# Gated spectral mix: t transform in four 32-row tiles, inverse d transform in two 64-row tiles, no regroupings, Mish table first, a new order

## The chip, the cores and the metric

The kernel runs on one core of a Trainium2 chip. The metric is the time of one execution in microseconds (us), the median of the runs; the profile is of one execution, and its times are told from the start of its span. TensorE (PE) multiplies, VectorE (DVE), ScalarE (ACT) and GpSimd (POOL) do the rest, and transfers (DMA) are issued from the queue of SyncE (SP) or of ACT. TensorE writes to PSUM, eight banks of 128 x 512 float32, and one of the other engines has to evict a bank before it can be written anew.

## What is computed

With S = 2048, D = 512, F = 1792 and one batch, all inputs in bfloat16:

```python
x = A_x
g = sigmoid((x * gate_w).sum(-1, keepdims=True))
X = rfft2(x.astype(float32), axes=(-2, -1)) * (A_w_r + 1j * A_w_i)     # 2048 x 257 filter weights
a = irfft2(X, s=(S, D), axes=(-2, -1)).astype(bfloat16)
h = einsum("bsd,df->bsf", x, B_w1) + B_b1
act = h * tanh(softplus(h))                                            # Mish
b = einsum("bsf,fd->bsd", act, B_w2)
return g * a + (1 - g) * b
```

(B_x is not used: the second branch takes x as well.)

## The kernel before

**Two branches, one written order.** Every step is a task with a name, made with `G.add` or `dma`; `ORDER` (L325) lists all tasks by name in one order, with the engine and the PSUM bank or scratch slot of those that have a choice (`t4_0::4` begins at bank 4, `sw4_0:dve:0` runs on DVE in slot 0). `place` (L219) deals them out to five queues in this order, and `emit` gives each task a wait for what it reads, and for what the last user of its bank or slot did. So each engine works off its queue strictly in the order of the text. The estimated durations in the code play no part in the program. A task of POOL also waits for the last DVE task marked `lock` that stands ahead of it in the order.

**Dense branch.** `m{c}_{ft}` (L853): for each of four chunks c of 512 rows and each of 14 feature tiles ft, four matmuls with 512 columns fill a bank, and ACT evicts it with Mish (`h{c}_{ft}`, L858). `n{t}` (L871): for each of 16 row tiles, 14 matmuls with 512 columns; `o{t}` (L885, L888) evicts them with the factor 1 - g. The transposed x that the m tasks read comes for tiles 0 to 7 from TensorE (`tr{t}`, `evx{t}`) and for 8 to 15 from transposing transfers (`xt{t}`).

**Spectral branch.** Rows are split as s = 16 p + t, and the 2-D transform is made in three products and back in three:

- butterflies of the two halves of d: `bf{a}_{uv}` (L574), on DVE or POOL;
- `p{t}` (L587): the transform over p, four 128-column matmuls for each t, evicted by `ep{t}` into `zu` (rC);
- `d{t}` (L598): the transform over d, likewise, evicted by `ed{t}` into rD;
- first regrouping: `s1w{g}` writes rD to a scratch in memory (four transfers of 512 KB), `s1r{g}` reads it back into `In` (rE), regrouped so that the 128 partitions hold (t, e, real or imaginary, c);
- `t{q}_{i}` (L705): the transform over t: for each of 64 slots f one matmul, 128 rows, with a matrix `Mm[:, f, :]` of its own (rF, loaded by `ldM{g}`); evicted by `et{q}` into `Y` (rC);
- the filter, for each group q of 8 slots: `sw{q}_{j}` copies Y with its partition halves swapped (L715, L716), `p1`, `p2`, `ad` (L723, L726, L729) multiply with `Wr` (rW) and `Wi` (rA) and add;
- the column k = 0 and the Nyquist column share one place; the products `e1` (L745, L746) and `e2` (L765, L767) and the small tasks es0, es1, xp1, xp2, ead, e3 filter them apart. `e1` reads all filtered groups of Y;
- `it{q}_{i}` (L783): the inverse over t, with `Gm` (rB, `ldG{g}`), evicted by `eit{q}` into `H` (rF);
- second regrouping: the twelve copies `hx` from `Hv` (rF) to `Dv` (rC), so that the 128 partitions hold both real and imaginary parts;
- `id{t}` (L827): the inverse over d, four matmuls with 128 rows for each t, evicted by `ec` (L834, L835) and two sums `ey` (L838) into `yb`;
- `ip{t}`: the inverse over p; for tiles 8 to 15 it is added in the bank of `n{t}` (L879, with g and 1/(1 - g) folded into its matrix, `rfs`), for 0 to 7 it has a bank of its own (L897) and `fin{t}` (L901) adds it.

**Filter weights.** `wr0s1`, `wi1s0` and the like load pieces of the 2048 x 257 weights from SP's queue to rS; eight moves for each of Wr and Wi (`wrm000` and so on, L638 on ACT, L640 and L641 on DVE or POOL), each of 32 partitions and 16 slots, put them in their layout, contiguous over k; `wrn0`, `wrn1` copy rW to its other half by a transfer, `win0`, `win1` (L651) do the same for Wi on DVE with a change of sign; `wrc`, `wrz`, `wic`, `wiz` set the shared column.

**The gate.** `gate0` and `gate8` (L676): 32 matmuls of one column each; `zcl`, `ez` (POOL), `ezb`, `ez1`, `omg`, `gc` make g and 1 - g. `zt` (L804) transposes a small piece of it, `zte` evicts that, and `zw`, `zr` spread it through memory.

Of the kernel before, what the change touches and what calls it, by code (L numbers as in the profile page):

```python
# [8 lines left out]
BF = mybir.dt.bfloat16  # L9
# [9 lines left out]
WP = 130  # L19
# [111 lines left out]
def _build_consts():  # L131
    R, FDm = _const_p(), _const_d()
    M, G = _const_t()
    front = np.concatenate([R[:, None, :], FDm], axis=1)
    inv = np.zeros((128, 5, 128))
    inv[:, 0] = R.T * (2.0 / (S * D))
    for uv in range(2):
        for e in range(2):
            for kri in range(2):
                inv[kri::2, 1 + 2 * uv + e] = FDm[:, 2 * uv + e, 64 * kri:64 * kri + 64].T  # L140
# [4 lines left out]
    return dict(front=front, inv=inv, edge=np.concatenate(edge, axis=1),  # L145
                M=M.transpose(1, 0, 2), G=G.transpose(1, 0, 2))
# [179 lines left out]
warm::0 wrp1 graw wrp0 x0 ones ident braw x2 ebase cRF w1_0 tr0::0 bf0_0:dve bf0_1:dve tr_b::1 tr1::2 evx0:act xt8 ev_b tr3::3 bf2_0:dve cFD bf2_1:dve  # L326
tr2::0 evx3:dve evx1:act p0::4 x4 evx2:dve p1 p2::6 ep0:act p3 m0_0::0 ep2:dve xt11 m0_2::1 h0_0 m0_1::6 w1_8 h0_2 bf4_1:dve tr7::7 h0_1 tr4::1 tr6::0
evx7:dve tr5::4 bf4_0:pool evx6:act d2::2 evx4:dve d3 evx5:dve wr1s1 m0_3::7 ed2:dve m1_1::6 h0_3 p4::2 w1_4 h1_1 p6::4 m0_13::7 m1_13::6 h0_13 wr0s2
p7 wr1s0 h1_13 m1_11::7 ep6:dve wr0s0 m0_11::6 h1_11 m1_6::4 h0_11 xt13 m0_7::5 wrm100:act wrm101:dve x8 m0_8::6 wrm111:dve wrm110:dve m0_5::7 xt9 h0_8
p5 h0_7 d6::0 ep4:dve d7 wi1s1 h0_5 m1_9::6 ed6:act bf8_1:pool m1_12::7 xt14 h1_9 d0::0 m0_4::5 h1_12 h1_6 ldM2 m0_10::7 bf8_0:dve h0_4 p8::2 x12 h0_10  # L330
p9 m1_8::5 ep8:dve d1 h1_8 m0_12::7 wi1s0 ed0:act d8::4 d9 p10::2 wr0s1 h0_12 p11 d4::0 m1_10::6 ep10:act bf12_1:dve gate0::7 ed8:act bf12_0:pool s1w0
d10::2 h1_10 zcl0 d11 m1_3::4 ed10:dve d5 h1_3 m0_6::6 ez0 ed4:dve wi0s1 wrm010:act wim111:pool p14::4 p15 m1_0::7 ez10 ep14:dve s1w1 p12::0 h1_0 p13
m0_9::2 ezb0 ep12:dve wip1 h0_6 wrm000:pool d14::4 wim100:act d15 m1_4::3 omg0 ed14:dve xt10 d12::0 d13 wip0 m1_7::6 h1_4 wrm011:dve s1w2 h0_9 m1_2::7
wrm001:dve h1_7 gc0 wim110:dve m1_5::2 ed12:act wim101:pool m2_0::6 xt12 h1_2 h1_5 m2_8::0 s1w3 m2_11::7 win1 m2_13::1 wic1:pool m2_7::2 s1r2 wiz1:dve
m2_2::3 wi0s0 m2_10::4 h2_11 m2_3::5 wi0s2 h2_13 s1r0 h2_2 m2_12::7 h2_7 m2_5::1 xt15 h2_12 wim010:dve h2_0 m2_6::2 wim011:dve h2_3 s1r3 m2_4::3 h2_6
wim001:dve s1r1 h2_5 m2_9::5 wim000:pool h2_4 gate8::1 h2_9 wrn0 h2_10 m3_13::3 zcl8 h2_8 win0 m3_2::2 h3_13 ldM0 m3_5::0 h3_2 wic0:pool wiz0:dve ez8
t4_0::4 ldG1 h3_5 t4_1 m3_3::2 ezb8 ez18 wrc0:pool et4:act omg8 wrz0:pool m3_11::3 w2_2 h3_3 sw4_0:dve:0 t1_0::4 sw4_1:dve h3_11 t1_1 m3_9::2 p2_4:dve
et1:act zt::3 t5_0::0 ldM1 zte m3_12::6 h3_9 sw1_1:act:1 t0_0::2 t0_1 zw m3_8::7 et0:dve h3_12 ldG2 sw1_0:act m3_6::4 sw0_1:dve:2 ldM3 h3_8 m3_10::5
p1_1:dve sw0_0:act p2_1:dve t2_0::6 t2_1 w2_0 m3_4::2 h3_6 ad_1:dve w2_8 h3_10 p1_0:dve m3_0::3 h3_4 p2_0:dve t3_0::4 h3_0 t3_1 et2:dve m3_7::2 ldG3
m2_1::3 et3:dve ad_0:pool h3_7 t6_0::6 h2_1 t6_1 wrn1 t5_1 sw2_0:dve:1 t7_0::4 sw3_1:act:2 sw2_1:dve t7_1 n3_0::3 et6:dve p1_2:pool et7:act zr rft  # L340
sw3_0:act inv et5:act p2_2:dve ldG0 n0_0::2 wrc1:dve o3_0:dve wrz1:pool edge rfs p1_4:dve ad_2:dve ad_4:dve sw7_1:act:1 n1_0::3 p1_3:dve sw5_0:act:0
sw7_0:dve p2_3:dve sw5_1:act p2_7:dve ad_3:dve o0_0:act n7_0::0 p2_5:dve sw6_1:act:2 p1_5:dve sw6_0:dve ad_5:dve p2_6:dve p1_6:dve n4_0::2 o7_0:act
p1_7:dve ad_6:dve ad_7:dve o1_0:dve e1::0 n2_0::3 o4_0:act xp1::1 es0::2 es1 xp2 ead::0 e2::2 m3_1::0 o2_0:act e3 it1_0::2 h3_1 it1_1 it0_0::4 eit1:dve
it0_1 it7_0::6 eit0:act it7_1 it3_0::0 it3_1 eit7:dve it5_0::2 eit3:act it5_1 it2_0::4 it2_1 eit5:act eit2:dve it4_0::6 it4_1 it6_0::0 it6_1 n5_0::2
eit6:act eit4:dve hx8_00 hx8_10 hx8_01 n6_0::3 o5_0:act hx8_11 hx0_01 hx4_11 hx4_10 hx0_00 id14::6 o6_0:dve id15 hx0_11 id12::0 ec14:act:0 id13 id10::4
# [8 lines left out]
def _build(nc, A_x, A_w_r, A_w_i, B_x, B_w1, B_b1, B_w2, gate_w, out, merge=8, xtp=8, NWARM=13):  # L354
# [6 lines left out]
    scr = nc.dram_tensor("scr", (NT, 4, 128, 128), BF)  # L361
# [4 lines left out]
    with es:  # L366
# [17 lines left out]
        wsr = sb("wsr", [128, 2, NF], BF)  # L384
        wsi = sb("wsi", [128, 2, NF], BF)
# [61 lines left out]
        scr_w = scr.rearrange("t r m k -> m (t r) k")  # L447
        scr_r = scr.rearrange("t r (c f) k -> (t r c) (f k)", c=2)
# [8 lines left out]
        def dma(name, dst, src, us, cls="dma", queue="sp", is_out=False, transpose=False, **kw):  # L457
# [7 lines left out]
            issue = 1.31 if transpose else dict(sp=0.6, act=0.4, pool=1.1)[queue]  # L465
            t = G.add(name, [(queue, issue, fn)], cls, **kw)
# [45 lines left out]
        G.add("warm", [("pe", NWARM * 0.213, f_warm)], "warm", writes=[wb])  # L512
        G.add("ones", [("pool", 0.2, lambda e: e.memset(identt[:, :], 1.0))], "small", writes=["ident"])
# [14 lines left out]
        for ri, (src, nm) in enumerate(((A_w_r, "wr"), (A_w_i, "wi"))):  # L528
            wv = src.rearrange("(q m) k -> q m k", m=128)
            for fh in range(2):  # L530
# [6 lines left out]
                for j, (pm, fs, ms, us) in enumerate(parts):  # L537
                    dma(f"{nm}{fh}s{j}", sg[pm:32:2, fs, :], wv[:, ms, :], us, writes=[(nm, fh, "s", j)])
# [40 lines left out]
        for t in range(0, NT, 2):  # L579
            b, b2 = _Buf("b2"), _Buf("b2")  # L580
            for i in range(2):
                def f_p(e, t=t + i, i=i, b=b):
# [8 lines left out]
            evac(f"ep{t}", lambda t=t: zu[:, :, t:t + 2, :], lambda b=b: pair(b).rearrange("p (t c f) -> p c t f", t=2, c=4), 1024,  # L591
                 [b], [("zu", t), ("zu", t + 1)], "p")
            for i in range(2):
                def f_d(e, t=t + i, i=i, b=b2):
                    ins = None
                    for c in range(4):
                        o = 256 * i + 128 * (c % 2)
                        ins = e.matmul(bank(b, c // 2)[:, o:o + 128], zu[:, c, t, :], FD[:, c, :], start=True, stop=True)  # L598
# [13 lines left out]
        dma("edge", rD[:, 7168:8192], d_edge[:].rearrange("p c m -> p (c m)"), 0.7, writes=["edge"], deps=t_s1w)  # L612
        for g in range(4):
            dma(f"ldM{g}", Mm[:, 16 * g:16 * g + 16, :], d_M[:, 16 * g:16 * g + 16, :], 1.4, writes=[("M", g)])
# [344 lines left out]
```

## Time and profile before

| | |
|---|---|
| median of 3 runs (lowest to highest) | 142.3 us (142.06 to 142.41) |
| span of the profiled execution, first to last instruction | 139.5 us |
| the time that lies around the span, from these two | 2.8 us |
| granted TensorE clock, mean | 1.000 |
| busy: PE, DVE, ACT, POOL | 128.4, 80.2, 79.6, 25.3 us |
| L853 (m), 224 matmuls of 512 columns | 52.1 us |
| L871 (n), 210 matmuls of 512 columns and 28 of 256: the groups that read hs, rD, rS | 24.9, 12.7, 12.9 us |
| L587, L598, L705, L783, L827, 64 matmuls of 128 columns each | 4.9, 5.2, 4.7, 4.1, 4.6 us |
| transfers | 23.57 MB in 23,870 packets |

Busy time of PE is the time in which at least one matmul is under way by the profile; single matmuls overlap (379 ns is the mean of one with 512 columns, and 216 ns the distance between the starts of two). The profiled execution has no time of its own beside its span; the median stands 2.8 us above it.

### The profile page before, as it was taken

What the parts mean: (1) busy time and instruction counts of PE and PEld (TensorE: products, weight loads), DVE (VectorE), ACT (ScalarE), POOL (GpSimd) and SP (SyncE); (2) the same over time, 40 slices, a digit from 0 to 9 for tenths busy, and PEclk for the clock granted to TensorE, in tenths of its full rate; (3) what the DMA queues carried; (4) which work ended last, traced back from release to release, by engine and by line L of the source; (5) the groups of instructions that cost most, each with busy time, mean ns of one, the idle gap of its engine ahead of it and who ended that gap; (6) DMA issues with size and microseconds to landing.
All of it is one profiled execution on the core that took longest, in us unless ns stands there. A gap on an engine that the chain in (4) does not pass through costs nothing.

```text
span 139.5 us, 2328 instructions
## 1 busy us (share of the span) xinstructions
PE 128.4 (92%) x918; PEld 70.0 (50%) x918; DVE 80.2 (58%) x121; ACT 79.6 (57%) x107; POOL 25.3 (18%) x27
## 2 busy tenths in 40 slices
PE   7989999999699996989959999499999999999992
PEld 5646445676344434454434444147648565444451
DVE  0665359529973034347993498945905669972220
ACT  3496699889980696989895069117714144000111
POOL 3023006089515005710361000000000000000000
DMA  4999999995959999999999500000075310050142
GB/s 106 300 309 227 252 214 171 350 192 130 212 114 249 237 162 335 303 370 280 310 305 215 194 5 0 0 5 0 0 297 192 136 37 1 5 207 18 75 153 94
DMA packets 23870, 23.57 MB, mean 169 GB/s; under 512 B 13940, under 2 KB 19956, under 8 KB 23540
## 3 DMA queue, kind: packets, MB, share of 16 engines
q1 hardware_dynamic: 23392, 23.20, 63.0%
q10 hardware_dynamic: 468, 0.23, 0.8%
q8 instruction: 7, 0.11, 0.3%
q14 instruction: 3, 0.02, 0.1%
HBM read 15.02 MB, written 4.20 MB: 138 GB/s over the span
## 4 chain that ended last, share of the span: by engine, by line
PE 52%; DMA 19%; DVE 12%; ACT 7%; SPq 6%; issue 2%; ACTq 0%
PE ps L871 24%; PE ps L853 14%; DMA rW<-rW 9%; DMA rF<-c_m 8%; SPq L463 5%; ACT tmp L716 3%; PE ps L827 3%; DMA w_sb<-in_B_b_dram 2%; PE ps L598 2%; DVE rC L729 2%; DVE rF L493 2%; DVE rD L493 2%; DVE rC L493 2%; PE ps L587 2%; ACT hs L858 1%
## 5 line engine op out<-in xcount | busy, mean ns | idle before, releaser
L853 PE MATMUL ps<-rX,w_sb 128*128 128x512 bf16 x224 | 52.1, 379 | 0.0
L853 PEld LDWEIGHTS ps<-rX,w_sb 128*128 128x128 bf16 x224 | 20.8, 98 | 21.2 <-ACT hs L858 0.4
L871 PE MATMUL ps<-w_sb,hs 128*128 128x512 bf16 x112 | 24.9, 379 | 2.0 <-ACT rC L496 1.8
L885 ACT ACTIVATE rX<-ps,omg 128x512 bf16<-128x512 f32 (+1 forms) x11 | 7.1, 648 | 26.2 <-PE ps L879 19.9
L858 ACT ACTIVATE hs<-ps,b1f 128x512 bf16<-128x512 f32 x28 | 18.2, 692 | 4.4 <-PE ps L853 4.3
L871 PEld LDWEIGHTS ps<-w_sb,hs 128*128 128x128 bf16 x112 | 10.7, 98 | 15.2 <-ACT rC L496 2.0
L493 DVE CAST rC<-ps 128x1024 bf16<-128x1024 f32 x10 | 12.1, 1221 | 7.6 <-PE ps L587 6.1
L716 ACT ACTIVATE tmp<-rC 64x1024 bf16<-64x1024 bf16 x9 | 9.5, 1055 | 6.4 <-DVE rC L729 6.2
L871 PE MATMUL ps<-w_sb,rS 128*128 128x512 bf16 (+1 forms) x70 | 12.9, 336 | 0.0
L871 PE MATMUL ps<-w_sb,rD 128*128 128x512 bf16 x56 | 12.7, 379 | 0.0
L858 ACT ACTIVATE rD<-ps,b1f 128x512 bf16<-128x512 f32 x14 | 8.4, 689 | 4.5 <-DMA scr<-rD 3.2
L858 ACT ACTIVATE rS<-ps,b1f 128x512 bf16<-128x512 f32 x14 | 9.3, 687 | 2.5 <-PE ps L853 2.3
L574 POOL TENSOR_TENSOR rB<-rA 128x1024 bf16<-128x1024 bf16 x3 | 6.4, 2120 | 21.8 <-DVE rB L574 11.7
L838 DVE TENSOR_TENSOR rA<-tmp,ps 128x512 bf16<-128x512 f32 x16 | 9.9, 682 | 0.4 <-PE ps L827 0.4
L888 DVE TENSOR_SCALAR rX<-ps,omg 128x512 bf16<-128x512 f32 x6 | 4.5, 748 | 8.6 <-PE ps L871 4.9
L871 PEld LDWEIGHTS ps<-w_sb,rS 128*128 128x128 bf16 x70 | 6.7, 98 | 4.8
L871 PEld LDWEIGHTS ps<-w_sb,rD 128*128 128x128 bf16 x56 | 5.5, 98 | 6.6 <-DVE rX L901 0.2
L574 DVE TENSOR_TENSOR rB<-rA 128x512 bf16<-128x512 bf16 (+1 forms) x7 | 5.0, 740 | 4.9 <-DMA rA<-in_A_x_dram 4.9
L834 ACT ACTIVATE tmp<-ps 128x512 f32<-128x512 f32 x7 | 4.0, 598 | 6.7 <-PE ps L827 6.6
L901 DVE SCALAR_TENSOR_TENSOR rX<-ps,gcol,rX 128x512 bf16<-128x512 f32 x8 | 5.6, 745 | 2.5 <-PE ps L897 2.5
L496 ACT ACTIVATE rC<-ps 128x1024 bf16<-128x1024 f32 x6 | 6.1, 1020 | 0.8 <-PE ps L705 0.4
L726 DVE TENSOR_TENSOR tmp<-tmp,rA 128x1024 bf16<-128x1024 bf16 x8 | 6.2, 787 | 0.1
(86 smaller groups left out, 144.3 us busy)
## 6 DMA issues: line engine op xcount, KB each, us to landing
w_sb<-in_B_w_dram SPq DMA_DIRECT2D x3, 768.0 KB, 8.1
rF<-c_m SPq DMA_DIRECT2D x4, 512.0 KB, 9.3
scr<-rD SPq DMA_DIRECT2D x4, 512.0 KB, 4.2
rE<-scr SPq DMA_DIRECT2D x4, 512.0 KB, 8.1
rB<-c_g SPq DMA_DIRECT2D x4, 512.0 KB, 9.4
out_dram<-rX SPq DMA_DIRECT2D x7, 256.0 KB, 2.0
rA<-in_A_x_dram SPq DMA_DIRECT2D x3, 512.0 KB, 8.5
rW<-rW SPq DMA_DIRECT2D x2, 520.0 KB, 11.4
```

The costliest lines, as they stand in the source:

```text
L463: return e.dma_start(a, b)
L493: return e.tensor_copy(out=o(), in_=i())
L496: return e.activation(o(), i(), AF.Copy)
L574: return e.tensor_tensor(out=xu[:, a:b_, uv, :], in0=x_sb[:, a:b_, 0:256], in1=x_sb[:, a:b_, 256:512], op=ALU.add if uv == 0 else ALU.subt ...
L716: ("act", act(1024), lambda e, z=z, lo=lo, i_=i_: e.activation(tb(z)[lo:lo + 64], i_, AF.Copy))],
L726: return e.tensor_tensor(out=zv(z), in0=zv(z), in1=Wi[:, fa:fb, 0:128], op=ALU.mult)
L838: return e.tensor_tensor(out=yb[:, t:t + 2, 256 * h:256 * h + 256].rearrange("p t (i e) -> p t i e", e=2), in0=t4(z), in1=o4(bank(b, 1)), ...
L853: ins = e.matmul(bank(b), w1_sb[:, dt_, 128 * ft:128 * (ft + 1)], xT[:, c, dt_, :, :], start=(dt_ == 0), stop=(dt_ == 3))
L858: G.add(f"h{c}_{ft}", [("act", act(512, 1), lambda e, c=c, ft=ft, b=b: e.activation(hs[c][:, ft, :], bank(b), AF.Mish, bias=b1f[:, ft:ft + ...
L871: ins = e.matmul(bank(b)[:, 0:hi - lo], hs[c][:, ft, 128 * tl:128 * (tl + 1)], w2_sb[:, ft, lo:hi], start=(ft == 0), stop=(ft == NFT - 1 a ...
L885: return e.activation(bs[:, t, lo:hi], bank(b)[:, 0:hi - lo], AF.Copy, scale=omg[:, t:t + 1])
L901: return e.scalar_tensor_tensor(out=bs[:, t, :], in0=bank(b), scalar=gcol[:, t:t + 1], in1=bs[:, t, :], op0=ALU.mult, op1=ALU.add)
```

## The change

- The rows of `In` are now (j, c, t) with j = f mod 4: each of the four 32-row tiles of the array takes one slot f, and what was one matmul of 128 rows for a slot is four of 32 rows, added up in the bank over a = (e, real or imaginary). A task `t{q}` has 64 matmuls for 16 slots and four banks, in the order g, a, j, so that neighbours go to different tiles and banks: 256 in all for 64 before. In this layout the transform over d can write it directly: `p` is evicted into `zu` with t innermost (`ep`), `d{g}` takes 128 columns of (8 slots of f, 16 t) and is evicted by `ed{g}` into `In`. `s1w`, `s1r` and the scratch are gone. A `d` task now reads what all `ep` tasks wrote.
- `id{t}` reads `Hv` where `it` left it: eight matmuls of 64 rows in two row tiles, for four of 128 rows. The `hx` copies are gone.
- A one-element Mish (`tab`) is the first task of ACT, and every Mish eviction depends on it.
- The moves of the filter weights write their columns regrouped (k u to u k, 132 columns a slot in place of 130), and read every second element for that. Four POOL memsets (`wrp`, `wip`) and the copies to `wsr`, `wsi` are gone; the shared column sits in column 65.
- `c0{q}`, four small DVE copies, keep the unfiltered shared column, and `e1` reads them; `e3` is written in four parts.
- Seven of the ten filter loads are issued from ACT's queue, the other three from SP's.
- `ORDER` is new: x0, x2, x4, x8 are loaded ahead of w1, the m tasks of all chunks lie around and behind the t tasks (23 of them between `t3` and `e1`), and n, id and ip follow.

The core of the diff (the two orders are cut down to their beginnings and the stretch around the t tasks, and the constants, which only follow the layout, are left out):

```diff
-WP = 130
+WP = 132
...
-warm::0 wrp1 graw wrp0 x0 ones ident braw x2 ebase cRF w1_0 tr0::0 bf0_0:dve bf0_1:dve tr_b::1 tr1::2 evx0:act xt8 ev_b tr3::3 bf2_0:dve cFD bf2_1:dve
...
-m2_1::3 et3:dve ad_0:pool h3_7 t6_0::6 h2_1 t6_1 wrn1 t5_1 sw2_0:dve:1 t7_0::4 sw3_1:act:2 sw2_1:dve t7_1 n3_0::3 et6:dve p1_2:pool et7:act zr rft
...
+x0 tab warm::0 ones ident x2 x4 bf0_1:dve tr0::1 bf2_0:pool tr2::2 evx2:dve cRF x8 graw tr3::3 braw w1_0 evx0:act bf4_0:pool evx3:act bf2_1:dve tr1::4
...
+m0_7::6 p5 ep4:act gate0::7 m0_6::3 m1_7::1 wr0s0:sp h0_7 bf12_1:dve h1_7 ebase zcl0 ez0 p8::4 m0_1::2 h0_1 wr0s1:act wr1s0:act wrm001:pool p9 p12::6
+p13 ep8:dve p14::0 wr1s1:act ldM0 p15 ep14:dve m1_6::2 m1_2::4 m0_9::5 ezb0 wrm101:pool ep12:act d2::0 d3 ed2:dve d4::6 h0_6 h1_6 h1_2 xt14 d12::2 d5
...
+wrm000:dve m1_13::5 m1_12::0 h1_12 m2_13::3 h2_13 et01:dve c00 m2_8::4 gate8::1 wim010:dve zcl8 ez8 h1_13 wim001:dve ldM2 win0 wrn0 sw01_1:dve:0
+wrc0:pool ldM3 t1::62 et11:act et10:act m1_1::0 h1_1 h2_8 m2_11::5 sw00_1:dve:1 h2_11 m3_1::1 m3_2::2 wrm100:dve t2::63 et21:act c01 m3_5::0 m1_8::5
+m2_1::3 wim110:dve wic0:pool wrn1 wim101:dve h3_2 ezb8 zt::4 win1 et20:act zte h1_8 sw00_0:dve ez18 sw01_0:dve h3_1 wrz0:dve m0_11::2 h0_11 t3::64
...
+        t_tab = G.add("tab", [("act", 1.4, lambda e: e.activation(junk[:, :], one[:, 0:1], AF.Mish))], "small", writes=["junk"])
...
-                    dma(f"{nm}{fh}s{j}", sg[pm:32:2, fs, :], wv[:, ms, :], us, writes=[(nm, fh, "s", j)])
+                    dma(f"{nm}{fh}s{j}", sg[pm:32:2, fs, :], wv[:, ms, :], us, queue="sp act", writes=[(nm, fh, "s", j)])
...
-            evac(f"ep{t}", lambda t=t: zu[:, :, t:t + 2, :], lambda b=b: pair(b).rearrange("p (t c f) -> p c t f", t=2, c=4), 1024,
+            evac(f"ep{t}", lambda t=t: zu.rearrange("p u f t -> p (u f) t")[:, :, t:t + 2], lambda b=b: pair(b).rearrange("p (t x) -> p x t", t=2), 1024,
...
-                    for c in range(4):
-                        o = 256 * i + 128 * (c % 2)
-                        ins = e.matmul(bank(b, c // 2)[:, o:o + 128], zu[:, c, t, :], FD[:, c, :], start=True, stop=True)
+                    o = bank(b, i).rearrange("p (e r u k) -> p u e r k", e=2, r=2, u=2)
+                    for uv in range(2):
+                        for e_ in range(2):
+                            c = 2 * uv + e_
+                            ins = e.matmul(o[:, uv, e_], rC[:, 2048 * c + 128 * g:2048 * c + 128 * (g + 1)], FD[:, c, :].rearrange("p (r k) -> p r k", r=2), start=True, stop=True)
...
-            t_s1w.append(dma(f"s1w{g}", scr_w[:, 16 * g:16 * g + 16, :], rD[:, 2048 * g:2048 * (g + 1)].rearrange("p (r k) -> p r k", k=128),
-                             2.4, "s1", reads=[("y1", 4 * g + i) for i in range(4)], writes=[("scr", g)]))
-        for g in range(4):
-            t_s1r.append(dma(f"s1r{g}", rE[g:128:4, :], scr_r[32 * g:32 * g + 32, :], 1.4, "s1", reads=[("scr", g)], writes=[("In", g)]))
...
-                            i_ = sg[:, 16 * h:16 * h + 16, 0:129] if pt == 0 else sg[:, 16 * h:16 * h + 16, 256:127:-1]
-                            o_ = dstv[base + 32 * pt:base + 32 * pt + 32, f0 + 16 * h:f0 + 16 * h + 16, 0:129]
+                            i_ = sg[:, 16 * h:16 * h + 16, 0:WP] if pt == 0 else sg[:, 16 * h:16 * h + 16, 256:256 - WP:-1]
+                            i_ = i_.rearrange("p f (k u) -> p f u k", u=2)
+                            o_ = dstv[base + 32 * pt:base + 32 * pt + 32, f0 + 16 * h:f0 + 16 * h + 16, :].rearrange("p f (u k) -> p f u k", u=2)
...
-                    for k in range(4):
-                        f = f0 + 4 * i + k
-                        ins = e.matmul(bank(b, i)[:, 128 * k:128 * (k + 1)], Mm[:, f, :], In[:, f, :], start=True, stop=True)
+                for g in range(4):
+                    for a in range(4):
+                        for j in range(4):
+                            r = slice(32 * j, 32 * j + 32)
+                            ins = e.matmul(bank(bp[j // 2], j % 2)[:, 128 * g:128 * g + 128], Mm[r, 4 * q + g, a, :], In[r, 4 * q + g, a, :],
+                                           start=(a == 0), stop=(a == 3))
...
-        G.add("e1", [("pe", 0.2, f_e1)], "edge", reads=yall + ["edge"], writes=[eb])
+        G.add("e1", [("pe", 0.2, f_e1)], "edge", reads=[("c0s", q) for q in range(4)] + ["edge"], writes=[eb])
...
-                    dma(f"hx{a}_{uv}{kri}", Dv[kri:128:2, uv, a:b_], Hv[uv:128:2, kri, a:b_], 0.3 * (b_ - a) / 4 + 0.1, "hx",
...
-                    for uv in range(2):
-                        for e_ in range(2):
-                            o = 256 * i + 128 * e_
-                            ins = e.matmul(bank(b, uv)[:, o:o + 128], Dv[:, uv, t, e_, :], cinv[:, 2 * uv + e_, :], start=True, stop=True)
+                    for e_ in range(2):
+                        o = 256 * i + 128 * e_
+                        for kri in range(2):
+                            for uv in range(2):
+                                r = slice(64 * uv, 64 * uv + 64)
+                                ins = e.matmul(bank(b, uv)[:, o:o + 128], Hv[r, kri, t, e_, :], cinv[r, 2 * kri + e_, :], start=(kri == 0), stop=(kri == 1))
...
-            dph = {0: [], 1: [], 2: t_s1w, 3: t_mv}[c]
+            dph = [t_tab] + (t_mv if c == 3 else [])
```

More of the change, by code (lines that the diff above doesn't have):

```diff
@@ L330 @@
[L330 to L337, printed above, removed]
@@ L342 @@
[L342 to L345, printed above, removed]
@@ L383, in _build @@
         tmp = sb("tmp", [128, 3, 1024], BF)
[L384 to L385 removed]
+        c0s = sb("c0s", [128, NF], BF)
         b1f = sb("b1f", [128, NFT], F32)
@@ L610, in _build @@
[L610 to L614 removed]
+            dma(f"ldM{g}", Mm[:, 4 * g:4 * g + 4, :, :], d_M[:, 4 * g:4 * g + 4, :, :], 1.4, writes=[("M", g)])
```

177 lines of the change are left out of this document (95 added, 82 removed).

## The prediction

> **What bounds the kernel now.** I read the head of the page, then the waits of TensorE, then the chain that ended last, then TensorE's timeline, then the groups by form. First the head:
>
> ```profile
> span 139.5 us, 2328 instructions
> PE 128.4 (92%) x918; PEld 70.0 (50%) x918; DVE 80.2 (58%) x121; ACT 79.6 (57%) x107; POOL 25.3 (18%) x27
> GB/s 106 300 309 227 252 214 171 350 192 130 212 114 249 237 162 335 303 370 280 310 305 215 194 5 0 0 5 0 0 297 192 136 37 1 5 207 18 75 153 94
> ```
>
> TensorE is the bound: every other engine is idle 40% of the time or more. The GB/s row says that transfers run at some 200 to 350 GB/s until 80 us and then nearly stop. So two things can change the time: how much TensorE has to do, and how long it stands. Where it stands:
>
> ```profile
> PE ps L745 <- issue: 1.9, 1, 1.9
> PE ps L871 <- ACT rC L496: 1.8, 1, 1.8
> PE ps L676 <- DMA rX<-in_A_x_dram: 1.2, 1, 1.2
> PE ps L598 <- DVE rC L493: 1.1, 2, 0.9
> PE ps L705 <- DMA rF<-c_m: 0.5, 1, 0.5
> PE ps L561 <- ACT hs L858: 0.4, 1, 0.4
> ```
>
> The columns are sum, times, longest. L745 is the first edge product e1, which waits for the whole filter. The chain that ended last shows why the filter was late:
>
> ```profile
> 48.85 10.80 DMA rF<-c_m
> 66.22 12.45 DMA rW<-rW
> ```
>
> A matrix load and a copy of the filter weights (rows of start and duration) each took over 10 us, behind the regroup traffic on the one queue of SP. Now TensorE's timeline, for prices:
>
> ```profile
> 53.47 0.94 PE L676 MATMUL ps<-gw_sb,rX 128*128 128x1 bf16 x32 [1.23 <-DMA rX<-in_A_x_dram]
> ...
> 61.11 0.22 PE L804 MATMUL ps<-identt,ezb 128*16 128x128 bf16 x1
> 61.27 0.40 PE L705 MATMUL ps<-rE,rF 128*128 128x128 bf16 x4
> ...
> 70.28 1.28 PE L705 MATMUL ps<-rE,rF 128*128 128x128 bf16 x20
> ```
>
> A full matmul with 128 columns: (1.28 - 0.22) / 19 = 56 ns. A matmul with one column, each with its own 128x128 weight load: (0.94 - 0.16) / 31 = 25 ns; that is how fast load-and-multiply pairs can follow one another when there is next to nothing to stream. L804 uses only a part of the array (16 weight columns): four 512-column matmuls of 0.216 us from 60.16 end at 61.02, it begins 0.09 later, and L705 follows 0.16 and not 0.06 behind it. So going into a part-array form and out again costs 0.19 us.
>
> TensorE's time, by starts: first real matmul at 3.9, last at 136.6, end of span 2.85 later. Dense work from first to last, with 0.216 and 0.056 us for 512 and 128 columns, is 121.9 us; so 10.8 us are waits. They are: front up to 10.1 us 1.1, the d transform 1.4, the second gate 1.4, the t transform's matrix loads 1.2, n3 behind an eviction 2.0, the edge products 2.6, and 1.1 in small pieces.
>
> **The change, part by part.**
>
> *TensorE work, t.* 64 matmuls at 56 ns (3.6 us) become 256 with 32 rows. No row has such a form. Bounds: 14 ns, if four row tiles run wholly side by side (56/4), and 56 ns, if they run one after another. I take 27 ns, because the nearest row is L676: weights of as many columns have to be loaded ahead of each of them, and pairs came no closer than 25 ns (its weight loads: 1.8 us for 64, 28 ns). 256 x 27 ns = 6.9 us: +3.3.
> The Trainium skill, "TensorE: Matmul & The Clock Gate", Part 3, says that matmuls on different row groups start some 4 ns apart. By that rule four of them take 56 + 3 x 4 = 68 ns, which makes 4.4 us (an estimate from the page) in place of 6.9. L676 shows 25 ns between starts, though on the whole array.
>
> *Inverse d.* 64 matmuls become 128 with 64 rows, bounds 28 (56/2) and 56 ns. I take 28, just over the same 25 ns: 3.6 us, +0.
>
> *Switches.* t lies in four blocks, inverse d in three: 7 x 0.19 = +1.4 us, bounds 0 and twice that.
>
> *Both regroupings.* s1w/s1r (2 MB out, 2 MB back) and the twelve hx copies leave SP's queue. The hx cost nothing before: n5 and n6 (28 matmuls, 6.1 us at L871) covered them. The four scratch writes and reads did cost, through what stood behind them: xt15, the ldM, the wrn copies. With them go the waits at the second gate (1.4) and at the matrix loads (1.2). Now d writes its 8 evictions straight into In, and t0 needs only the first two.
>
> *New order, front.* x4 and x8 go ahead of the first part of w1 on SP. In the trace x0 landed at 3.9 and x4 at 8.6, with 1.44 MB behind x0: 0.30 MB per us, as the GB/s row. With x2, x4, x8 and w1_0 behind x0 (1.84 MB) the first w1 lands at 3.9 + 6.1 = 10.0. TensorE has 3.7 us to do before m0_0 (8 transposes, 8 p) and could begin it at 7.6: 2.4 us of waiting, against 1.1 now. Afterwards p12 to p15 wait for x12 (1.0 MB later, 13.5) and a POOL butterfly of 2.12 us, ready at 15.6; TensorE gets there at 17. ACT now issues seven filter loads, 0.6 us each by the SP rows, with Mish evictions queued behind them, and TensorE behind those. Adding up ACT from m0_1 on (three issues, ep12, h0_6, h1_6 at 0.65, 1.02, 0.69, 0.69) puts h1_6 at 21.7, where d12 wants its bank at 21.0: 0.7. So the front costs 3.1, with the d transform's 1.4 within it.
>
> *Mish table first.* One table load of 1.28 us leaves 7.5 us on ACT and goes under the first x load. The 0.4 us of L561 behind L858 go; counted above.
>
> *Middle.* From t0 (34 us) to e1 (73 us) TensorE has 39 us of work, ACT 29 and DVE some 34. e1 no longer reads the filtered Y but c0s, four small copies, so the 2.6 us of waiting at the edge go if the filter is ready when e2 comes, at 76. DVE's chain: zte at 50.4, then 22 us of swaps, products and sums, with 1.3 us lost to POOL's two ad, gives ad_30 at 73, ead at 74.5. It holds with 2 us to spare. n3's 2.0 us go as well, since 23 Mish tiles now lie between t3 and n1. POOL's filter moves start at 22, when the loads issued by ACT have landed, and end at 42, before win1 wants them.
>
> *Filter moves on DVE.* They now read every second element (k u to u k). Bounds for one: 0.70 us as now, and 2.5 at one element a step:
>
> ```profile
> L641 DVE TENSOR_SCALAR rW<-rS 32x2064 bf16<-32x2064 bf16 x3 | 2.0, 696 | 0.1
> L493 DVE CAST rC<-ps 128x1024 bf16<-128x1024 f32 x10 | 12.1, 1221 | 7.6 <-PE ps L587 6.1
> ```
>
> The second row is 1.19 ns an element, times 2112. I take 1.3, about half of it, as the two-source products do (687 ns for 1024): no row has this order. Eight moves: +4.8 us of DVE, hidden, since DVE waits for the second gate and for zt; without that cover up to 4.8 us.
> The Trainium skill, "VectorE: DVE Perf Modes", What auto-detection actually checks, speaks against these moves: pairing needs a step of one, so they fall from four elements a cycle to two. That would be 1.2 to 1.3 us (an estimate), no other than the value taken.
>
> *End of it, small things.* it7 to it4 share banks with evictions: 0.4. The ep evictions write runs of two elements; L493 and L496 wrote runs of 8 (rF) and 1024 (rD) at the same 1.2 and 1.0 us, so nothing; the bound is twice that for eight of them, 1 to 2 us before d2. c0s, e3 in four parts: 0.6 us of DVE under n1. Four POOL memsets go, off the path. Small pieces 0.6 as now, and the tail 2.85 as now, since an out of 64 KB still ends it.
>
> *Sum.* Work +3.3 + 1.4 = +4.7. Waits: 3.1 + 0.4 + 0.6 = 4.1 in place of 10.8, -6.7. Together -2.0: span 137.5 us. The median of the runs lies 2.8 us above the profiled span (142.3 against 139.5); with the same, 140.3 us.
>
> **The rivals.**
>
> *B, the row tiles run wholly side by side.* 14 ns, so t costs 3.6 and not 6.9: 134.2, median 137.0. For it: the tiles have rows and banks of their own. Against it: 25 ns in L676. By the skill's 4 ns it would be 135.0, an estimate.
>
> *C, they do not overlap* (the change does not do what it says). t +7.4 and inverse d +3.6 over my sum: 148.5, median 151.3. It decides from 35 ns a matmul on (2.0 us / 256 above 27). For it: no matmul in the trace overlaps another's streaming, 512 columns always cost 216 ns. Against it: the built program gives the tiles row positions 0, 32, 64 and 96.
>
> *D, slow filter moves.* At 2.5 us, four of them (wim001, wrm100, wim110, wim101) stand between the second gate and zte on DVE, 4 x 1.2 = 4.8 us late. t3 takes zt's bank and so waits for zte, and h3_2 on ACT, whose target held the staged weights, waits for the last move; there is 0.9 us to spare. TensorE stands 3.9 us: 141.4, median 144.2, slower. It decides from about 1.5 us a move on.
>
> **How the numbers follow.** About 0.3% (0.4 us) can be told from no change. Forecast 0.50, B 0.13, C 0.15, D 0.14, other stalls of over 1.6 us in front or on ACT 0.08. The forecast has 0.44 of faster, 0.04 of same and 0.02 of slower, as its waits are good to some 1.5 us; the last case 0.03 of same and 0.05 of slower. Faster 0.57, same 0.07, slower 0.36. The range begins at B, 137.0, takes in D and the part of C up to 147.0 (switches at twice the price, tiles that overlap by half), and leaves out full C and a little more.
>
> **What would show it.** Right: the 256 t matmuls in four blocks of about 6.9 us in all, no wait at e1 or n1, the first m tile at 10 us, filter moves of about 1.3 us. Wrong: blocks of 3.6 us each (C) or of 1 us (B), t3 behind zte (D), many short waits for Mish evictions behind ACT's own issues.

## The result, and the profile after

The changed kernel takes 149.7 us (median of 4 runs, 147.9 to 153.0) beside 142.3 us of the kernel before on the same chip: ratio 1.043, 95% interval 1.037 to 1.049. It is slower by some 4%, where 140.3 us was forecast. The ratios given here leave disturbed runs out, so that they are not quite the quotients of the medians. The profiled execution took 148.3 us, with a span of 146.3 us where 137.5 was forecast.

The head of the page of the changed kernel:

```profile
span 146.3 us, 2775 instructions
PE 129.9 (89%) x1158; PEld 72.2 (49%) x1174; DVE 97.2 (66%) x131; ACT 65.9 (45%) x97; POOL 40.7 (28%) x30
...
PEclk9995999999999995599999999999999999999999
...
GB/s 118 288 349 218 291 192 256 182 291 167 76 139 157 0 39 226 50 283 357 402 64 0 4 0 0 0 4 0 0 54 4 0 0 0 4 73 142 72 143 90
```

The transfers are fewer (17.32 MB for 23.57) and the GB/s row has gaps from 37 us on: the regrouping traffic is gone, as the change says. But DVE has 17.0 us more to do and POOL 15.4, and the granted clock of TensorE falls twice to about a half: in the slice from 11.0 to 14.6 us, and in the two from 54.9 to 62.2 us. The waits of TensorE, and one of ACT (sum, times, longest; lines of the changed kernel, where L593 is p, L860 m, L809 zt, L706 t, L834 id, L865 Mish):

```profile
PE ps L809 <- DVE ezb L688: 5.1, 1, 5.1
PE ps L593 <- DVE rB L580: 2.4, 1, 2.4
PE ps L860 <- DVE rC L498: 1.3, 1, 1.3
...
PE ps L593 <- POOL rB L580: 0.7, 1, 0.7
```

```profile
ACT rS L865 <- DVE rA L640: 6.5, 1, 6.5
```

The waits that the forecast removed (second gate, matrix loads, n3, edge products) are gone. In their place stand zt, which waits 5.1 us for a small DVE cast (ezb), two p tasks behind butterflies (L580), and an m task behind the t eviction et30. TensorE's timeline shows what was paid and what was gained:

```profile
10.52 0.86 PE L593 MATMUL ps<-w_sb,rB 128*128 128x128 bf16 x8 [2.36 <-DVE rB L580]
...
12.27 1.91 PE L593 MATMUL ps<-w_sb,rB 128*128 128x128 bf16 x16
14.29 0.81 PE L860 MATMUL ps<-rX,w_sb 128*128 128x512 bf16 x3
...
37.77 1.07 PE L706 MATMUL ps<-rE,rF 32*128 32x128 bf16 x64
39.00 3.40 PE L860 MATMUL ps<-rX,w_sb 128*128 128x512 bf16 x15 [0.16 <-issue]
...
56.52 0.27 PE L809 MATMUL ps<-identt,ezb 128*16 128x128 bf16 x1 [5.08 <-DVE ezb L688]
57.03 1.89 PE L860 MATMUL ps<-rX,w_sb 128*128 128x512 bf16 x4 [0.24 <-ACT rS L865]
58.85 1.89 PE L706 MATMUL ps<-rE,rF 32*128 32x128 bf16 x64
...
97.97 1.51 PE L834 MATMUL ps<-rE,rF 64*128 64x128 bf16 x48
```

A block of 64 row-tile matmuls takes 1.07 us with its last one's 0.21: 14 ns each, a quarter of 56. The record of the first matmul behind each such block is missing (15 are shown at 39.00 for 16 in the program, 11 at 48.90 for 12), and so is one at 14.29 (3 for 4; in all L860 has 224 weight loads on record and 215 matmuls), so that the rows there begin later than the work did. The 16 matmuls at 12.27 should take 0.9 + 0.2 us and take 1.9, the four at 57.03 take 1.89 for 1.03: half the clock, behind a wait.

DVE's and POOL's timelines show why DVE was late. First DVE, then POOL:

```profile
7.52 2.95 DVE L580 TENSOR_TENSOR rB<-rA 128x1024 bf16<-128x1024 bf16 x2 [0.87 <-DMA rA<-in_A_x_dram]
...
37.59 1.88 DVE L689 TENSOR_SCALAR gcol<-zcl 128x8 f32<-128x8 f32 x1
39.38 1.24 DVE L640 COPY rW<-rS 32x2112 bf16<-32x2112 bf16 x1
40.55 1.21 DVE L498 CAST rC<-ps 128x1024 bf16<-128x1024 f32 x1
...
43.99 2.71 DVE L640 COPY rA<-rS 32x2112 bf16<-32x2112 bf16 x1
46.81 2.83 DVE L651 TENSOR_SCALAR rA<-rA 64x4224 bf16<-64x4224 bf16 x1
...
55.00 1.25 DVE L640 COPY rA<-rS 32x2112 bf16<-32x2112 bf16 x1
56.28 0.18 DVE L688 CAST ezb<-zcl 128x8 bf16<-128x8 f32 x1
...
61.89 5.00 DVE L736 TENSOR_TENSOR tmp<-tmp,rA 128x1024 bf16<-128x1024 bf16 x2
```

```profile
7.56 2.62 POOL L580 TENSOR_TENSOR rB<-rA 128x1024 bf16<-128x1024 bf16 x1 [1.19 <-DMA rA<-in_A_x_dram]
...
32.41 1.96 POOL L641 TENSOR_SCALAR rW<-rS 32x2112 bf16<-32x2112 bf16 x1
...
42.53 3.06 POOL L641 TENSOR_SCALAR rW<-rS 32x2112 bf16<-32x2112 bf16 x1
45.67 2.86 POOL L641 TENSOR_SCALAR rA<-rS 32x2112 bf16<-32x2112 bf16 x1
```

A filter move takes 1.25 us on DVE and 1.96 on POOL when the other engine is quiet. Side by side each waits for the other's end. The plainest case is L689, a small operation of the gate that takes 0.17 us when POOL is quiet (58.24): begun at 37.59 beside a POOL move of 37.48 to 39.44, it ends at 39.47. POOL's move of 42.53 ends at 45.59; DVE's, queued at 43.99, ends at 46.70, 1.11 behind that; POOL's next one ends at 48.53, 1.83 behind that; DVE's L651 ends at 49.64, 1.11 behind that: each takes little less than its time alone once the other has ended. Only DVE's evictions out of PSUM (40.55, 1.21 us beside a POOL move) run on undisturbed. The Trainium skill states this: "SBUF — State Buffer", section SBUF: two separate sides, says that GpSimd and the operations of VectorE that use the second pair of ports share that pair as an exclusive lock, which whoever comes first holds for the whole instruction. The trace agrees, with the ends above.

Against the forecast, by four places that it named:

| | forecast | measured | late |
|---|---|---|---|
| first m tile | 10.0 | 13.9 | 3.9 |
| t0 | 34 | 37.8 | 3.8 |
| e1 | 73 | 82.6 | 9.6 |
| end of span | 137.5 | 146.3 | 8.8 |

So 3.8 us were lost ahead of t0, 5.8 more between t0 and e1, and nothing behind e1. (The first m tile has its first weight load at 13.87; the first of its matmuls on record is its second.) The middle: zt's wait 5.1, the lowered clock behind it 2.4 (1.0 in the four m matmuls, 0.8 in t3, 0.6 in the m matmuls that follow), et30 1.3, small pieces 0.3, less some 0.8 for each of the four t blocks, which cost 1.1 with their switches where 1.9 was forecast.

### The profile page after: what moved, and what is told of

The parts are those of the page before. It is cut to its first block, busy times and chain, and to the rows that moved or that the text cites. A ratio compares the mean times of both kernels' runs of the same rounds, so it can differ in the third digit from the quotient of the medians.

```text
span 146.3 us, 2775 instructions
## 1 busy us (share of the span) xinstructions
PE 129.9 (89%) x1158; PEld 72.2 (49%) x1174; DVE 97.2 (66%) x131; ACT 65.9 (45%) x97; POOL 40.7 (28%) x30
## 2 busy tenths in 40 slices
DMA packets 14463, 17.32 MB, mean 118 GB/s; under 512 B 5428, under 2 KB 11444, under 8 KB 14260
## 4 chain that ended last, share of the span: by engine, by line
PE 74%; DVE 15%; DMA 4%; issue 4%; ACT 1%; SPq 1%; DVEq 0%
PE ps L878 33%; PE ps L860 26%; DMA rA<-in_A_x_dram 4%; PE ps L593 3%; DVE rA L640 3%; PE ps L834 3%; PE ps L794 2%; PE ps L608 2%; DVE rB L580 2%; DVE rA L641 2%; DVE tmp L724 2%; DVE rW L640 2%; DVE rC L498 2%; DVE gcol L689 1%; PE ps L706 1%
## 5 line engine op out<-in xcount | busy, mean ns | idle before, releaser
L860 PE MATMUL ps<-rX,w_sb 128*128 128x512 bf16 x215 | 51.0, 386 | 2.7 <-DVE rC L498 1.3
L860 PEld LDWEIGHTS ps<-rX,w_sb 128*128 128x128 bf16 x224 | 21.2, 100 | 25.5 <-DVE rC L498 1.8
L865 ACT ACTIVATE hs<-ps,b1f 128x512 bf16<-128x512 f32 x28 | 18.1, 686 | 8.1 <-PE ps L860 6.2
L501 ACT ACTIVATE rC<-ps 128x1024 bf16<-128x1024 f32 x10 | 10.5, 1056 | 8.6 <-PE ps L593 3.8
L865 ACT ACTIVATE rS<-ps,b1f 128x512 bf16<-128x512 f32 x14 | 9.2, 691 | 7.5 <-DVE rA L640 6.5
L865 ACT ACTIVATE rD<-ps,b1f 128x512 bf16<-128x512 f32 x14 | 9.2, 689 | 5.6 <-PE ps L860 5.6
L580 DVE TENSOR_TENSOR rB<-rA 128x1024 bf16<-128x1024 bf16 (+1 forms) x7 | 6.6, 967 | 5.4 <-DMA rA<-in_A_x_dram 5.4
L498 DVE CAST rC<-ps 128x1024 bf16<-128x1024 f32 x6 | 7.1, 1218 | 3.7 <-PE ps L593 3.7
L498 DVE CAST rE<-ps 128x1024 bf16<-128x1024 f32 x5 | 5.9, 1221 | 5.5 <-PE ps L608 5.5
L498 DVE CAST rF<-ps 128x1024 bf16<-128x1024 f32 x5 | 5.9, 1221 | 4.7 <-PE ps L794 4.7
L593 PE MATMUL ps<-w_sb,rB 128*128 128x128 bf16 x64 | 5.8, 249 | 3.1 <-DVE rB L580 2.4
L736 DVE TENSOR_TENSOR tmp<-tmp,rA 128x1024 bf16<-128x1024 bf16 x7 | 8.4, 1216 | 0.1
```

The costliest lines, as they stand in the source:

```text
L498: return e.tensor_copy(out=o(), in_=i())
L501: return e.activation(o(), i(), AF.Copy)
L580: return e.tensor_tensor(out=xu[:, a:b_, uv, :], in0=x_sb[:, a:b_, 0:256], in1=x_sb[:, a:b_, 256:512], op=ALU.add if uv == 0 else ALU.subt ...
L593: ins = e.matmul(bank(b, i)[:, 128 * c:128 * (c + 1)], xu[:, t, uv, e_:256:2], RF, start=True, stop=True)
L736: return e.tensor_tensor(out=z3(z), in0=z3(z), in1=wi3, op=ALU.mult)
L860: ins = e.matmul(bank(b), w1_sb[:, dt_, 128 * ft:128 * (ft + 1)], xT[:, c, dt_, :, :], start=(dt_ == 0), stop=(dt_ == 3))
```

## The experiments

Three theories stand against each other: DVE and POOL hold one another up, and what is late on DVE is what TensorE waits for (theory of the trace); the order alone is at fault, each wait for itself; the regrouped moves alone are too slow. All kernels are the changed one with the edit shown, except in run 10. They ran on several chips, where the kernel before took 141.0 to 142.4 us; so runs are compared by their ratios to the kernel before on the same chip, and the changed kernel stands at 1.043.

**1. bf0_0 straight behind bf0_1.** The p tasks waited 2.4 us for a butterfly queued behind others on DVE.

```diff
-... bf4_1:dve bf0_0:dve ep2:act ...
+... bf0_1:dve bf0_0:dve tr0::1 ...
```

> One token of the order moved: bf0_0 directly behind bf0_1 on DVE, and no longer behind bf4_1, which waits for x4. Theory F (the front is lost to the order of DVE's queue): p0 has its butterflies some 3 us earlier, TensorE no longer stands 2.4 us at L593, the clock isn't taken back at 10 to 14 us, and m0_0 begins at 11 us or before instead of 14.3: 2.5 to 4 us less. Rival (the front is bound by the transfers of x): p0 comes earlier, but p10 and m0_0 wait for x8 and w1 as before, m0_0 at 13 us or later, under 1 us gained.

145.9 us (145.8 to 146.0), ratio 1.034 (1.028 to 1.040); span 143.9. The wait at L593 for DVE falls from 2.4 to 0.4 us, the first m tile comes at 11.7 and t0 at 35.3; zt still waits 5.2. How much of this is the edit's depends on what it is set against: with the front unchanged t0 begins at 37.8 in the changed kernel's profile, but at 36.2 in those of runs 2 and 3, on the same chip as this run, where L593 waits 1.8 and 1.0 us and the granted clock does not fall in the front. So the place of one butterfly cost 0.9 to 2.4 of the front's 3.8 us, less than the 2.5 to 4 of theory F.

**2. zt later.** The m2 tiles ahead of the m3 tiles that wait for the moves, and ezb8, zt and zte behind m2_12 with another bank.

```diff
-... h3_2 ezb8 zt::4 win1 et20:act zte ...
+... m2_12::6 ezb8 zt::7 zte ...
```

> Only the order: the tiles m3_1, m3_2, m3_5 change places with m2_4, m2_9, m2_5 (so no Mish eviction of chunk 3, which waits for all filter moves, stands before t3), and ezb8, zt, zte go behind m2_12, in bank 7. Theory M (the filter moves are late on DVE, and zt and h3_2 hand that to TensorE): the 5.1 us of waiting at zt, the clock loss behind it and the late h3_2 go, 5 to 8 us less, unless the same work is then late at e2. Rival (the filter chain sets the end wherever zt lies): TensorE stands as long at m2_12's bank or at e2 instead, under 2 us gained.

149.7 us (148.2 to 150.5), ratio 1.056 (1.044 to 1.068). The wait at zt is gone, and one in another place is larger:

```profile
PE ps L860 <- DVE rC L498: 8.7, 1, 8.7
```

That is m2_12, whose bank et30 has to free, and et30 stands behind filter tasks on DVE, with the two products of 2.5 us among them. The rival held: moving one wait on PE's queue gives nothing while DVE is late.

**3. Contiguous moves.** The filter moves do not regroup their columns (k u is kept), so the filter is applied with its columns in another order.

```diff
-                            i_ = i_.rearrange("p f (k u) -> p f u k", u=2)
```

> The 16 filter moves read and write contiguous columns (the regrouping of the columns is left out, everything else is as in the changed kernel). Theory S (the moves are late because they read every second element): a move on DVE falls from 1.25 to 0.70 us and on POOL not at all, zt's wait falls from 5.1 to 1 us or less. Theory P (DVE and POOL slow each other down): moves on DVE that run beside one of POOL still take 2 us or more, L651 and the swaps too; five moves by 0.55 us make 2.8 us before zt, so zt still waits 2 us or more and 2 to 3 us are gained.

144.9 us (143.4 to 146.0), ratio 1.018 (1.009 to 1.027); span 141.4. A DVE move falls to 0.71 us when alone, and zt's wait to 1.7, between what the two theories had (1 or less, 2 or more). Beside POOL a move still takes 1.71 us, L651 2.82 and the two products 4.99, and et30's wait is 1.5. So the cost of reading every second element and POOL's moves both lie behind zt's wait, and neither theory is enough by itself.

**4. POOL's moves cut to one slot of 16.** 15 of 16 slots of POOL's moves are left out (the weights there are cleared at the start); DVE's moves stay as they are.

```diff
-                            i_ = sg[:, 16 * h:16 * h + 16, 0:WP] if pt == 0 else sg[:, 16 * h:16 * h + 16, 256:256 - WP:-1]
+                            i_ = sg[:, 16 * h:16 * h + n, 0:WP] if pt == 0 else sg[:, 16 * h:16 * h + n, 256:256 - WP:-1]
...
+                        f_g = lambda e, op=op: op(e, False, 1)
...
-[("pool", 1.95, f_e),
+[("pool", 1.95, f_g),
```

> POOL's eight filter moves take one slot of sixteen each (the rest of the weights that POOL moves is left out; rW is cleared beforehand). Theory P (DVE and POOL slow each other down while both work in SBUF): all DVE moves take 1.25 us, L651 1.25 and the swaps 0.42 until 56 us, zt waits under 1 us, 5 to 8 us less in all. Theory S (the order of reading): DVE's times stay as they are without POOL's moves and zt waits 4 us or more.

143.6 us (142.5 to 146.2), ratio 1.015 (1.006 to 1.025); span 140.5. With POOL quiet the same DVE lines, which are L643 and L655 here, read

```profile
43.01 1.25 DVE L643 COPY rA<-rS 32x2112 bf16<-32x2112 bf16 x1
44.37 1.25 DVE L655 TENSOR_SCALAR rA<-rA 64x4224 bf16<-64x4224 bf16 x1
```

for 2.71 and 2.83 us. ezb comes 13.2 us behind the start of t0 on TensorE (37.36 to 50.51) in place of 18.5 (37.77 to 56.28). TensorE has 13.7 us to do from t0 to zt, so zt does not wait, and the granted clock is 1.000. This shows the cause of the 5.1 us: without POOL beside it DVE is in time, with its moves at 1.25. The two products of 2.5 us stay, beside POOL's p2 and ad, and et30's wait grows to 3.0; so the ratio falls by 0.028, some 4 us, and not by the 5 to 8 us of theory P.

**5. Row tiles one after another.** Within a t task the four matmuls that add up in one place are neighbours.

```diff
-                    for a in range(4):
-                        for j in range(4):
+                    for j in range(4):
+                        for a in range(4):
```

> The 64 matmuls of a t task in another order: the four matmuls of one 32-row tile, which add up in one place of one bank, stand next to each other, and the tile changes after each four. Everything else as in the changed kernel, and all of the computation is kept. Theory 1 (row tiles overlap only where neighbours in the queue go to different tiles): in place of 14 ns a matmul, three of four cost up to 56 ns, so a block takes up to 64 x (3 x 56 + 14) / 4 = 2.9 us in place of 1.07, four blocks up to 7.3 us more. Theory 2 (the array keeps several tiles busy whatever the order, since matmuls are queued some way ahead): blocks of 1.1 to 1.5 us, the time as the changed kernel.

```profile
36.37 1.12 PE L706 MATMUL ps<-rE,rF 32*128 32x128 bf16 x64
```

1.12 us for 1.07; 147.3 us in 2 runs, ratio 1.040 (1.026 to 1.054). Theory 2: the order of the tiles hardly matters. The records do not name the tile, so it stays open whether TensorE runs ahead to the next tile, or whether a 32-row matmul costs 14 ns by itself.

**6. p2_00, ad_00 and ad_01 on DVE.**

```diff
-wiz0:pool p2_00:pool ad_00:pool
+wiz0:pool p2_00:dve ad_00:dve
```

> p2_00, ad_00 and ad_01 run on VectorE in place of GpSimd; all of the computation is kept. Theory 1 (VectorE and GpSimd slow one another when both work in SBUF): VectorE's two products at L736 that took 2.5 us each beside GpSimd take about 0.7, which gives back 3.6 us and costs three operations of 0.7 us: et30 comes some 1.5 to 2 us earlier, its bank wait at L860 (1.3 us) goes, 1 to 1.5 us less than the changed kernel; the wait for zt (5.1 us) stays. Theory 2 (the long products are long for a reason of their own, such as their operands' layout): they stay at 2.5 us, VectorE has 2 us more to do and et30 comes 2 us later: 1 to 2 us more.

```profile
L736 DVE TENSOR_TENSOR tmp<-tmp,rA 128x1024 bf16<-128x1024 bf16 x8 | 5.4, 688 | 0.5 <-POOL rA L661 0.4
```

In the changed kernel these were 7 in 8.4 us, 1216 ns on average; now 8 take 5.4, and the wait for et30 falls to 0.4. So the long products were long through POOL's two operations, and DVE does three more tasks in less time. The total did not settle it: 147.9 us (145.3 to 150.0), ratio 1.032 (1.016 to 1.049), not to be told from the changed kernel, since zt still waits, 6.7 us in the profiled run.

**7 and 8. All repairs of the order.** bf0_0, the m2 tiles, the three DVE tasks, et30 right behind t3, zt behind m2_12, wrm100 on ACT. In 8 besides n0 ahead of e2.

```diff
-... wrm100:dve t2::63 ... wic1:pool ad_01:pool wiz1:pool ad_11:dve et30:dve ...
+... wrm100:act t2::63 ... t3::64 et31:act et30:dve ... wic1:pool ad_01:dve wiz1:pool ad_11:dve ... m2_12::6 ezb8 zt::7 zte ...
```

> All repairs of the order that the traces point to, with all of the computation kept: bf0_0 straight behind bf0_1; the m2 tiles that GpSimd's moves do not hold back ahead of the m3 tiles; p2_00, ad_00, ad_01 on VectorE and wrm100 on ScalarE; et30 right behind t3; zt and zte behind m2_12 in another bank; omg0 earlier. Theory 1 (the loss is the sum of separate waits, each with a cause of its own, front 2.4 to 3, zt 5 with 2 to 3 us of lowered clock behind it, et30 1.3): without them the span is 146.3 - 2.4 - 7 - 1.3 = some 135.5 to 138, a median of 138.5 to 141, below the kernel before. Theory 2 (TensorE waits for the filter chain on VectorE as a whole, and a wait removed in one place comes back in the next, at t3, e1 or e2): the span stays at 142 to 146, with the waits at e1 or e2 in place of zt's.

> As the kernel with all repairs of the order, and besides n0 and its eviction stand ahead of e2, so that TensorE has 14 more matmuls (3.0 us) to do before it needs the end of the filter chain; all of the computation is kept. Theory 1 (separate waits): no wait was left at e2, so the time is that of the repaired order, within 0.5 us. Theory 2 (the filter chain on VectorE is the bound): up to 3 us less than the repaired order alone.

7 took 144.4 us (143.7 to 145.2), ratio 1.022 (1.011 to 1.032); 8 took 150.6 (150.3 to 150.7), ratio 1.064 (1.055 to 1.072). In both zt still waits 4.8 us: ezb8 had been moved along with it, behind the filter tasks on DVE. And in 8 the evictions o1 and o0 stood on ACT ahead of es1, so that the edge products on DVE waited 7.3 us for an ACT that waited for n0. Both are misplacements of the experiment, so that the two theories were not decided here, and both say the same as the change itself: on an engine that works in the order of its queue, one small task in the wrong place stops another engine.

**9. As 7, with ezb8 early, zte behind ad_00, n4 ahead of e2.**

```diff
-... ez18 sw01_0:dve ... ezb8 zt::7 zte ...
+... ez18 ezb8 sw01_0:dve ... zt::7 zte sw11_1:dve ...
-... es1 xp1::2 xp2 ead::0 e2::5 ...
+... es1 n4_0::4 xp1::2 xp2 ead::0 e2::5 ...
```

> The repaired order once more, with what its trace showed: ezb8 is issued early, right behind ez18, so that zt no longer stands behind the filter tasks on VectorE; zte comes right behind ad_00, where zt is ready; n4 with its 14 matmuls (3.0 us) goes ahead of e2, with its eviction behind es1. All of the computation is kept. Theory 1 (separate waits): zt's 4.8 us go, nothing new is late at e2, since VectorE's chain ends at some 80 and TensorE arrives there at 76.7 + 3.0: span 142.0 - 4.8 = 137.2, median 139.5 to 140.5, ratio 0.98 to 0.99 against the kernel before. Theory 2 (the filter chain on VectorE is the bound, and the wait comes back at e2 or at the it tasks): span 140 to 142, no faster than the kernel before.

142.4 us (140.9 to 144.1, 12 runs), ratio 1.006 (1.002 to 1.010); span 139.2. zt's wait went, but 3.2 us came up at L860: sw31_1, a swap on ACT, waited 4.3 us for DVE with Mish evictions behind it. It is no faster than the kernel before, as theory 2 had it, but the wait is in neither of the places that this theory named.

**10. The kernel before, with the Mish table first.** The one part of the change that stands by itself.

> The kernel before with one part of the change alone: the one-element Mish as ScalarE's first task, with every Mish eviction behind it; all of the computation is kept. Theory 1 (as the prediction has it): the table load of 1.28 us leaves ScalarE's path at 7.5 us and the 0.4 us at L561 behind L858 go, 0.3 to 0.5 us less. Theory 2 (TensorE waits there for x and w1 from memory anyway): no difference above 0.3%.

143.0 us (142.3 to 144.1), ratio 1.014 (1.008 to 1.019): slower by 1.4%, where neither theory had it. In its profile the first transposes wait 1.1 us for the bias load (0.2 before), and n3 waits for w2 from memory:

```profile
PE ps L873 <- DMA w_sb<-in_B_w_dram: 3.6, 1, 3.6
```

Before, n3 waited 1.8, for an ACT eviction. Why those two transfers land later is not shown; ACT issues the bias load 0.05 us later than before.

**11 and 12. As 9, with the swap sw31_1 on DVE, and then sw10_1 too.**

```diff
-... wrz1:pool sw31_1:act ... ad_31:dve sw10_1:act:2 ...
+... wrz1:pool sw31_1:dve ... ad_31:dve sw10_1:dve:2 ...
```

> The repaired order with one more edit: sw31_1, a swap that stood on ScalarE's queue and waited 4.3 us there for a scratch slot of VectorE, with the Mish evictions h1_11, h2_6 and h3_13 and so TensorE (3.2 us at L860) behind it, runs on VectorE. All of the computation is kept. Theory 1 (separate waits): the 3.2 us go, VectorE's chain ends 0.4 us later, at 78.8, where TensorE now arrives at 81.7 - 3.3 = 78.4: span 136 to 136.8, median 137.7 to 139, ratio 0.97 to 0.98 against the kernel before. Theory 2 (the filter chain on VectorE is the bound): the wait comes back at e2, span 138.5 to 139.5, ratio about 1.0.

> The repaired order with the next swap on ScalarE's queue, sw10_1, on VectorE too: it waited 5.0 us there for VectorE's L739, with five Mish evictions and so TensorE (3.3 us at L860) behind it. All of the computation is kept. Theory 1 (separate waits): the 3.3 us go, VectorE's chain ends 0.4 us later, the sum ead at some 79.9, TensorE arrives at e2 at 82.0 - 3.3 = 78.7 and waits 1.2 us: span 139.5 - 2 = 137.5, median 139.2 to 140, ratio 0.98 against the kernel before. Theory 2 (the wait only moves along the filter chain): the same 3 us turn up at e2 or at an it task, span 139 to 140.

11: span 139.5, 141.2 us for the profiled execution (6 runs 140.6 to 144.9, no ratio on record). The same wait, at the next ACT swap:

```profile
PE ps L860 <- ACT rS L865: 3.3, 1, 3.3
```

12: 139.3 us (138.8 to 140.3, 12 runs), ratio 0.990 (0.985 to 0.994).

```profile
span 137.4 us, 2791 instructions
...
PE ps L774 <- DVE tmp L767: 1.4, 1, 1.4
```

The wait that is left is e2's for the end of DVE's chain, 1.4 us for the 1.2 expected, and the clock is 1.000. This version is 1.0% faster than the kernel before, and by the ratios some 5% faster than the changed kernel. The tiles, the missing regroupings and the direct filter layout were all kept; what changed are places in the order and the engine of six tasks.

## Why the prediction was wrong

**The step that failed** is "Eight moves: +4.8 us of DVE, hidden", and with it "It holds with 2 us to spare". The size of a move was right (1.3 forecast, 1.24 to 1.26 measured alone), though the row that it was taken from, 687 ns for 1024, gives 1.4 for 2112. But DVE's chain was added up as if POOL's moves did not touch it. From 37.6 to 52.1 us five groups of DVE took 6.8 us more than when alone (ez1 of the gate 1.7, the edge copy c0s 0.4, a move 1.5, L651 1.6, two swaps 1.6). zte was forecast at 50.4, 16.4 behind t0, and came 19.9 behind it: 3.5 us late, the last 0.9 of them behind an L651 that zt had not to wait for. Of zt's wait of 5.1 us some 2.4 are TensorE's own gain, since three t blocks of 1.1 us in place of 1.9 bring it to zt that much earlier; the other 2.7 are DVE's lateness. Runs 3 and 4 show DVE's side: cheaper moves take the wait down to 1.7 us, a quiet POOL takes all of it away.

**Only for ad_00 and ad_01** did the text see that POOL costs DVE something, 1.3 us. It was 2 x (2.5 - 0.69) = 3.6 us, and fell on two products ahead of et30. Run 6 shows that.

**The front.** Forecast: 2.4 us of waiting for w1, m0_0 at 10.0. Measured: 13.9, and no wait for w1 at all. TensorE waited for butterflies, 2.4 us for DVE's and 0.7 for POOL's; bf4_1 and bf0_0 on DVE took 2.95 us beside a POOL butterfly, for the 1.28 of the next two without one. The step that failed here reckoned with transfers alone, and not with the order of DVE's queue or with POOL beside it. Run 1 gives 0.9 to 2.4 us back. d12's 0.7 did not occur.

**t was mis-sized**: 27 ns from the row of one-column pairs, 14 measured. Rival B had it. In a group of four the starts of single matmuls lie some 3, 4 and 3 ns apart, and the next group follows some 46 ns later, 56 in all. The row of the Trainium skill ("TensorE: Matmul & The Clock Gate", Part 3, starts some 4 ns apart) agrees within a group; the 4.4 us estimated from it took 68 ns a group, and the four blocks take 3.6 us at full clock. L676's 25 ns, on the whole array, said nothing of row tiles. Inverse d was right at 28 ns. So were the switches, which the missing records hide in the changed kernel's rows. In run 4's profile all are there:

```profile
37.36 1.07 PE L710 MATMUL ps<-rE,rF 32*128 32x128 bf16 x64
38.37 3.63 PE L864 MATMUL ps<-rX,w_sb 128*128 128x512 bf16 x16
```

The first m matmul follows the start of t0 by 1.01 us, 0.90 of work and 0.11 for going out; going in costs some 0.1 more: 0.2 for 0.19.

**The lowered clock was not in the sum.** It cost some 1.6 us in the front (from 10.52 to 14.29 us TensorE did 2.1 us of work in 3.8) and 2.4 behind zt.

**Right**: the gone waits at the second gate, matrix loads, n3 and edge; the bandwidth set free; the size of a move; the price of a switch; nothing lost behind e1. (The GB/s row was misread: 7 of its slices up to 80 us lie under 200, from 106 to 194. Nothing hangs on it.)

**The rivals.** D named the right places: zt waits and h3_2 on ACT waits for the last move (6.5 us). Its reason, 2.5 us a move by the order of reading, was not the cause. B and D came true together. They had been taken as exclusive, though one is on TensorE and the other on DVE, and B makes D dearer. The range had room for each alone; the result has both, with POOL's hold on DVE, the front and the lowered clock besides, and lies outside it.

## What to carry to other kernels

Before work is called hidden on DVE, look at what GpSimd does in the same stretch: copies and two-source operations in SBUF on the two add up rather than overlap, so the cover has to hold the sum of both. A wait that is removed comes back at the next task behind the same late engine (zt, then et30, then two ACT swaps, then e2), so follow the late engine's chain to its end and move the small tasks out of its queue. And price a long wait of TensorE at more than its length: behind the 5.1 us the matmuls ran at a lowered clock, which cost 2.4 us more.

## What was not expected of the hardware

- Four row tiles of 32 rows run at 14 ns a matmul with 128 columns, and two of 64 rows at 28. For the 32-row tiles the order hardly matters (1.07 and 1.12 us for 64); for the others it was not tried.
- DVE and POOL take turns: 1.25 us becomes 2.71 and 2.83, 0.69 becomes 2.5, and POOL's 1.96 becomes 2.86 to 3.06; a DVE read of PSUM (1.21 us) is not held up.
- The clock after a wait. Behind every wait of 3.6 us or more the row of granted clock shows slices at 0.5 to 0.8 (the changed kernel, runs 1, 2, 5 to 8 and 10); behind waits of 3.0 to 3.3 us (runs 4, 9, 11) it shows none. The Trainium skill, "TensorE: Matmul & The Clock Gate", Part 1, has an idle window of some 3.4 us for that. The long waits fit it. But the row also fell behind shorter ones: 2.4 us with 0.7 and 0.2 ahead of it (the front of the changed kernel), 1.7 us with 0.3 and 0.5 after it (run 3), 2.2 us (run 8), and 0.7 us with 1.2 ahead of it (the front of run 9). So the length of one wait does not decide by itself, and what does stays open. Nor does the row show every slow stretch: in run 10 the 16 p matmuls at 6.84 us take 1.91 us, as those at 12.27 in the changed kernel do, with a granted clock of 1.00.
